# The second batch's attention on 64x64 matmuls, with its x read back from DRAM

## Chip, cores and metric

The kernel runs on one core of one Trainium2 chip. The metric is device time in microseconds, the median of several executions of the whole program.

## What is computed

Linear attention, then two dense layers, in float32. The inputs have 8 batches of 576 tokens and 8 heads of 64.

```python
kv = einsum('bhsd,bhse->bhde', k, v)
out = einsum('bhsd,bhde->bhse', q, kv)
x = out / sqrt(mean(out*out, axis=-1) + 1e-6) * g_norm     # to 4608 tokens x 512
x = square(maximum(x @ moe_w_in, 0)) @ moe_w_out           # 512 -> 2048 -> 512
h = x @ moe2_w_in
y = (h * cos(h)) @ moe2_w_out
```

## The kernel before, in words

A large matmul is made of three matmuls on operands that are split into a high and a low part (`h` by a cast to the matmul's reduced type, `l` by a subtraction): high by high, high by low, low by high.

The first layer's first part goes over tiles of `TOK` = 512 tokens, `t` = 0 to 8, and in each over 8 **chunks** of 128 hidden units, numbered through as chunk 0, 1, 2 and so on. `layer_in` (L370) computes a chunk's hidden units with 12 matmuls of 128x512 (L379); ScalarE and VectorE apply relu and square and split the result (`act_relu2`, its relu at L388 frees the PSUM bank `l`, its last step at L394 makes `gl`); two chunks later `layer_out` (matmuls L416) multiplies by the second weights, again 12 matmuls. So a chunk is 24 matmuls. The rest of the program (the other hidden units of layer one, and layer two, lines from 430 on) begins after these chunks.

Attention is computed batch by batch between the chunks. For batch `b`, 40 small matmuls (`kv_mm`, L258) make `kv`. Then come 8 **units** `(b, p, i)`: `p` is one of 4 pairs of heads. `att_a` (L278) multiplies q by kv into two `o` banks, `att_o` squares (L299) and scales (L300), `att_b` sums the squares over a head with a matmul by ones into the bank `ss` and takes the reciprocal root (L319, L321), `att_c` makes the normalized piece `xo` with three VectorE operations (L329 to L331), and `att_e` (L351) writes `xo` to DRAM (`x_d`) on GpSimd's queue. There are two ways through this:

- For `b < NEXACT` (before: batches 0 and 1) `att_a` uses one block-diagonal 128x128 float32 matmul for each half of the tokens (L288), and `att_b` one float32 matmul (L314). `att_d` (L334) casts and splits `xo` directly into `xh`, `xl` of the first `NDIRECT` tiles (L348, L349).
- For later batches `att_a` uses four 64x64 matmuls for each `p` (L292), one for each quarter of the array: two heads by two halves of the tokens. `sq` is split into `sh` and `sl` (L306, L307), and `att_b` takes two matmuls in the reduced type (L316, L317). `load_x` (L224) reads x back from `x_d` in two halves of the model dimension, `q` = 0 and 1, into a tile `xraw`, and `split_x` (L229) casts and splits it in four pieces `c` of 512 columns (L232, L233).

A table of jobs says after which chunk number each piece is asked for: `starts` gives, for each batch, the chunk number of its first unit and the step between units (L730); `at(n0 - ..., load_x, ...)` and `at(..., split_x, ...)` do so for x (L744 to L749). A scheduler then orders the instructions of each engine; each engine keeps that order, and a DMA queue issues in order too.

Of the kernel before, what the change touches and what calls it, by code (L numbers as in the profile page):

```python
# [8 lines left out]
F32 = mybir.dt.float32  # L9
# [7 lines left out]
P = 128  # L17
# [5 lines left out]
def kernel(  # L23
# [17 lines left out]
    NKC = DM // P  # L41
    NF = wA.shape[0]
    NH = NF // 2
    NP = NH // 2
    NEXACT = 2
    NQ = 3
    NRAW = 4
    KVB = 5
# [4 lines left out]
    TOK = 512  # L53
# [2 lines left out]
    TILES = [(0, 512), (BIG, 512), (2 * BIG, 512), (3 * BIG, 384), (3 * BIG + 768, 384)]  # L56
    assert sum(2 * ht for _, ht in TILES) == NT
    LAG = 2
    NDIRECT = 2
    EPS = 1e-6  # L60
    NSC = (S + P - 1) // P
    NPR = 7
# [28 lines left out]
    def bank(use):  # L91
        tag = banks[use].pop(0)
        banks[use].append(tag)
        return bank_tile(tag)

    def as32(ap):
        return ap.bitcast(F32)
# [111 lines left out]
    xraw = {}  # L209
# [6 lines left out]
    def pieces(first, count, size):  # L216
        done = 0
        while done < count:
            b, s = divmod(first + done, size)
            n = min(count - done, size - s)  # L220
            yield b, s, done, n
            done += n

    def load_x(t, q):  # L224
        raw = xraw[t, q] = x_p.tile([P, 2, TOK], F32, tag="xr", name="xraw", bufs=2)
        for b, s, done, n in pieces(t * TOK, TOK, S):
            nc.sync.dma_start(out=raw[:, :, done:done + n], in_=x_d[b][:, 2 * q:2 * q + 2, s:s + n])

# [49 lines left out]
    def att_a(*u):  # L278
# [6 lines left out]
        os = [bank("o")[:, :HS] for _ in range(2)]  # L285
        if b < NEXACT:
            for o, half in zip(os, halves):
# [8 lines left out]
    def att_o(o, *u):  # L296
# [3 lines left out]
        nc.scalar.activation(out=og, in_=o, func=AF.Copy, scale=gcol)  # L300
        if u[0] < NEXACT:
            att[u] = (og, sq, None)
# [7 lines left out]
    def att_b(*u):  # L310
        og, sh, sl = att[u]
        ss = bank("ss")[:, :HS]
        if u[0] < NEXACT:
            nc.tensor.matmul(ss, as32(ones[:]), sh[:], start=True, stop=True)  # L314
# [19 lines left out]
    def att_d(*u):  # L334
        b, p, hf = u
        xo = att[u]
        if b >= NEXACT:
            return
        tok = b * S + hf * HS
        for t in range(NDIRECT):  # L340
            lo, hi = max(tok, t * TOK), min(tok + HS, (t + 1) * TOK)
# [9 lines left out]
    def att_e(*u):  # L351
        b, p, i = u
        xo = att.pop(u)
        if b < NEXACT:
            nc.gpsimd.dma_start(out=x_d[b][:, p, i * HS:(i + 1) * HS], in_=xo)
# [319 lines left out]
    def at(n, fn, *a):  # L675
        jobs.append((n, len(jobs), fn, a))
# [50 lines left out]
    late_stream.place([pos(n) for n in (0.95, 2.5, 3.25, 4.5, 6.4, 8.7, 10.75)], 0)  # L727

    kv_stream = Stream(load_kv, kv_mm, [(b, c) for b in range(B) for c in range(NSC)])
    starts = [(-13, 1), (-3, 0.8)] + [(-3 + 7 * (b - 1), 7 / (2 * NKC)) for b in range(2, B)]  # L730
    kv_stream.place([s0 - 0.5 for s0, _ in starts for c in range(NSC)], 0)
    q_items = [(b, p) for b in range(B) for p in range(NKC)]
    for b, (s0, ds) in enumerate(starts):
        for i, u in enumerate(att_units(b)):
# [8 lines left out]
            at(n + 2.5, att_e, *u)  # L743
    for t in range(NDIRECT, NTILE):  # L744
        n0 = t * NH
        for q in range(2):
            at(n0 - (6.2, 3 if t == 2 else 4.2 if t == 3 else 5.1)[q], load_x, t, q)
        for c in range(NKC):
            at(n0 - 3.2 + 0.8 * c, split_x, t, c)  # L749


    PH = 1 / 7
# [184 lines left out]
```

## Time and profile before

| | |
|---|---|
| Median of 3 runs | 1575.07 us (1573.13 to 1575.84) |
| The profiled execution's own time | 1573.13 us |
| Its span, first to last instruction | 1571.4 us |
| TensorE busy in the span | 1536.6 us (98%) |
| VectorE, ScalarE, GpSimd busy | 82%, 68%, 7% |
| Mean granted TensorE clock | 0.998 |

The profiled execution is 1.94 us shorter than the median. Matmul times in the rows overlap, since one starts before the one ahead of it has ended: what a matmul costs is read from start to start, not from its duration. A float32 matmul stands as two instructions in the trace, so that "x2" can be one matmul. In a row of the timeline the brackets tell how long the engine was idle before it, and who ended that.

### The profile page before, as it was taken

The numbers are of one execution on the slowest core, as the hardware profiler recorded it, in microseconds if no ns is written. First come the engines' busy times: TensorE is split into PE (matmuls) and PEld (weight loads), VectorE is DVE, ScalarE is ACT, GpSimd is POOL, SyncE is SP. The second block draws the span as 40 slices with busy tenths as digits, with TensorE's granted clock in tenths as the row PEclk, the third lists the DMA queues.
The fourth block names the chain that finished last, engine by engine and source line by source line (L and its number), as shares of the span: only waits on it lengthen the run. The fifth ranks groups of instructions, "written<-read, shape, count | busy, mean of one in ns | idle before, by whom it ended". The sixth has DMA issues, their size and how long they took to land.

```text
span 1571.4 us, 24645 instructions
## 1 busy us (share of the span) xinstructions
PE 1536.6 (98%) x9104; PEld 1347.5 (86%) x9104; DVE 1294.0 (82%) x1744; ACT 1074.5 (68%) x1528; POOL 108.4 (7%) x171
## 2 busy tenths in 40 slices
PE   5999999999999999999999999999999999999998
PEld 4777777778888888888998899999999999999998
DVE  7987878888875899998979779867986788779777
ACT  5977767785434766656556777777777777777774
POOL 1112111110000000000000000000000000001000
PEclk9999999999999999999999999999999999999999
DMA  9858888877578979898997978887888789999995
GB/s 320 283 161 234 273 266 249 251 215 225 170 235 282 334 241 370 304 382 281 383 351 279 343 215 255 254 282 215 255 248 282 215 248 276 305 322 292 303 308 149
DMA packets 222151, 426.31 MB, mean 271 GB/s; under 512 B 18000, under 2 KB 138064, under 8 KB 222032
## 3 DMA queue, kind: packets, MB, share of 16 engines
q1 hardware_dynamic: 210560, 390.13, 73.2%
q0 software_dynamic: 11472, 34.61, 10.3%
q8 instruction: 73, 1.20, 0.3%
q14 instruction: 46, 0.38, 0.1%
HBM read 317.72 MB, written 81.79 MB: 254 GB/s over the span
## 4 chain that ended last, share of the span: by engine, by line
PE 80%; DVE 8%; DMA 7%; ACT 3%; issue 2%; SPq 0%; POOL 0%; DVEq 0%; ACTq 0%; POOLq 0%
PE SB L629 15%; PE FA L505 15%; PE FB L505 15%; PE SA L629 15%; PE acc L416 10%; PE l L379 8%; DMA ws_d<-raw 2%; DMA wi<-wi_d 1%; PE o L379 1%; PE ss L379 1%; DVE gl L606 1%; DMA xraw<-x_d 1%; DMA q<-in_qT 1%; DVE sum L657 1%; DMA sum<-part 1%
## 5 line engine op out<-in xcount | busy, mean ns | idle before, releaser
L505 PE MATMUL FA<-xh,wi 128*128 128x512 f32 (+1 forms) x840 | 302.7, 371 | 3.9 <-DVE h L534 2.8
L505 PE MATMUL FB<-xh,wi 128*128 128x512 f32 (+1 forms) x840 | 301.8, 370 | 0.0
L629 PE MATMUL SA<-ws,gh 128*128 128x256 f32 x1008 | 233.1, 280 | 0.4 <-ACT y L564 0.4
L629 PE MATMUL SB<-ws,gh 128*128 128x256 f32 x1008 | 233.1, 280 | 0.2 <-ACT part L654 0.2
L629 PEld LDWEIGHTS SA<-ws,gh 128*128 128x128 f32 x1008 | 183.6, 188 | 13.3 <-ACT y L564 0.5
L629 PEld LDWEIGHTS SB<-ws,gh 128*128 128x128 f32 x1008 | 183.3, 188 | 12.2 <-ACT part L654 0.4
L505 PEld LDWEIGHTS FA<-xh,wi 128*128 128x128 f32 x840 | 157.6, 189 | 14.2 <-DVE h L534 3.1
L505 PEld LDWEIGHTS FB<-xh,wi 128*128 128x128 f32 x840 | 157.3, 188 | 9.6
L606 DVE TENSOR_TENSOR gl<-y,gh 128x1024 fp32r<-128x1024 f32 (+1 forms) x100 | 111.5, 1114 | 40.5 <-ACT gh L605 40.3
L629 PE MATMUL SB<-ws,gl 128*128 128x256 f32 x504 | 141.3, 280 | 1.1 <-DVE gl L606 1.1
L629 PE MATMUL SA<-ws,gl 128*128 128x256 f32 x504 | 141.2, 280 | 0.5 <-DVE gl L606 0.5
L572 DVE SCALAR_TENSOR_TENSOR y<-y,h 128x1024 f32<-128x1024 f32 (+1 forms) x80 | 89.2, 1115 | 47.5 <-ACT y L568 47.3
L655 POOL DMA_DIRECT2D sum<-part x53 | 45.7, 862 | 1140.6 <-DMA ws<-ws_d 584.4
L554 ACT ACTIVATE y<-h,zerob 128x1024 int32<-128x1024 f32 (+1 forms) x80 | 85.0, 1063 | 50.3 <-DVE h L530 50.3
L416 PE MATMUL acc<-gh,wh 128*128 128x512 f32 x288 | 113.6, 396 | 0.0
L416 PE MATMUL acc<-gl,wh 128*128 128x512 f32 x288 | 112.9, 392 | 0.0
L416 PE MATMUL acc<-gh,wl 128*128 128x512 f32 x288 | 112.6, 391 | 0.0
L505 PE MATMUL FA<-xl,wi 128*128 128x512 f32 (+1 forms) x300 | 111.0, 370 | 0.0
L505 PE MATMUL FB<-xl,wi 128*128 128x512 f32 (+1 forms) x300 | 110.9, 370 | 0.0
L629 PE MATMUL SA<-gh,ws 128*128 128x512 f32 (+1 forms) x280 | 101.0, 369 | 0.6 <-ACT xh L478 0.6
L564 ACT ACTIVATE y<-y 128x1024 f32<-128x1024 f32 (+1 forms) x80 | 78.1, 976 | 34.0 <-DVE y L558 33.9
L629 PEld LDWEIGHTS SB<-ws,gl 128*128 128x128 f32 x504 | 94.9, 188 | 7.4 <-DVE gl L606 1.5
(171 smaller groups left out, 3820.6 us busy)
## 6 DMA issues: line engine op xcount, KB each, us to landing
wi<-wi_d SPq DMA_DIRECT2D x210, 512.0 KB, 6.4
ws<-ws_d SPq DMA_DIRECT2D x210, 512.0 KB, 5.3
sum<-part POOLq DMA_DIRECT2D x33, 512.0 KB, 7.3
kvld<-in_kv SPq DMA_DIRECT2D x32, 512.0 KB, 6.3
ws_d<-raw SPq DMA_DIRECT2D x24, 448.0 KB, 4.2
q<-in_qT SPq DMA_DIRECT2D x32, 288.0 KB, 4.8
p_d<-ev SPq DMA_DIRECT2D x18, 512.0 KB, 4.0
raw<-in_wA SPq DMA_DIRECT2D x16, 512.0 KB, 7.2
```

The costliest lines, as they stand in the source:

```text
L379: nc.tensor.matmul(ps, a[:, 0, cs], m[:], start=(c == 0 and k == 0), stop=(c == NKC - 1 and k == 2))
L416: nc.tensor.matmul(o, a[:, cs], m[:], start=(f == 0 and n == 0), stop=(f == NH - 1 and n == 2), skip_group_check=True)
L505: nc.tensor.matmul(ps[:, pp, :], a, b, start=(n == 0 and (i in (0, 2) or i == 1 and not seeded(k))), stop=(n == 5), skip_group_check=True,)
L554: nc.scalar.activation(out=y.bitcast(I32), in_=hs[k, b], func=AF.Identity, bias=zerob)
L564: nc.scalar.activation(out=y, in_=y, func=AF.Sin, scale=math.pi)
L572: nc.vector.scalar_tensor_tensor(out=y, in0=y, scalar=-2.0 * math.pi, in1=hs.pop((k, b)), op0=ALU.add, op1=ALU.mult)
L606: nc.vector.tensor_tensor(out=l, in0=src, in1=as32(h), op=ALU.subtract)
L629: nc.tensor.matmul(ps[:, b, :], lhs, rhs, start=(n == 0 and (m == 0 or b % 2 == 0) and i in (0, 1, 2)), stop=(n == 5), skip_group_check=True,)
L655: nc.gpsimd.dma_start(out=e, in_=part, accum_op=ALU.add)
L657: nc.vector.tensor_tensor(out=e, in0=ps, in1=e, op=ALU.add)
```

## The change

`NEXACT` and `NDIRECT` go from 2 to 1: batch 1 takes the 64x64 way, and the second tile's x (`t` = 1) is read back from `x_d` and split by `split_x`. Its `xraw` lies in the pool `ev`, which otherwise serves the results of `layer_out`. Batch 1's units are asked for 0.75 chunks apart instead of 0.8; batch 2 starts at chunk 5.5 with a step of 0.65, where it started at chunk 4 with 0.875. The loads of x get other leads for the tiles 1 and 2, and the four splits of every tile are asked for 2.4, 1.8, 1.2 and 0.6 chunks ahead of the tile, where they were asked for 3.2, 2.4, 1.6 and 0.8 ahead.

```diff
-    NEXACT = 2
+    NEXACT = 1
-    NDIRECT = 2
+    NDIRECT = 1
...
     def load_x(t, q):
-        raw = xraw[t, q] = x_p.tile([P, 2, TOK], F32, tag="xr", name="xraw", bufs=2)
+        if t == NDIRECT:
+            raw = ev_p.tile([P, 2, TOK], F32, tag="ev", name="xraw")
+        else:
+            raw = x_p.tile([P, 2, TOK], F32, tag="xr", name="xraw", bufs=2)
+        xraw[t, q] = raw
...
-    starts = [(-13, 1), (-3, 0.8)] + [(-3 + 7 * (b - 1), 7 / (2 * NKC)) for b in range(2, B)]
+    starts = [(-13, 1), (-3, 0.75), (5.5, 0.65)] + [(-3 + 7 * (b - 1), 7 / (2 * NKC)) for b in range(3, B)]
...
         for q in range(2):
-            at(n0 - (6.2, 3 if t == 2 else 4.2 if t == 3 else 5.1)[q], load_x, t, q)
+            lead = {1: (5.5, 3.2), 2: (5.6, 3), 3: (6.2, 4.2)}.get(t, (6.2, 5.1))
+            at(n0 - lead[q], load_x, t, q)
         for c in range(NKC):
-            at(n0 - 3.2 + 0.8 * c, split_x, t, c)
+            at(n0 - (2.4, 1.8, 1.2, 0.6)[c], split_x, t, c)
```

The lines of the changed file lie 4 or 5 further down: L292 of before is L296 there, L388 is L392, L416 is L420.

The scheduler's order of the instructions shows what moves. The first place is TensorE between the second product of chunk 4 and the first of chunk 6, where one head pair of batch 2 is multiplied. Before:

```order
L416 MATMUL acc_805<-gl,wh 128x512
L416 MATMUL acc_805<-gh,wl 128x512
L292 MATMUL l_1109<-q,kvx_137 64x288
L292 MATMUL o<-q,kvx_137 64x288
L292 MATMUL l_1109<-q,kvx_137 64x288
L292 MATMUL o<-q,kvx_137 64x288
L416 MATMUL acc_793<-gh,wh 128x512
```

With the change:

```order
L296 MATMUL l_1182<-q,kvx_137 64x288 x2
L420 MATMUL acc_816<-gh,wh 128x512
L383 MATMUL l_1094<-xh,wh 128x512
L383 MATMUL l_1094<-xl,wh 128x512
L320 MATMUL ss<-sh,ones 128x288
L420 MATMUL acc_816<-gl,wh 128x512
L420 MATMUL acc_816<-gh,wl 128x512
L296 MATMUL o<-q,kvx_137 64x288
L383 MATMUL l_1094<-xh,wl 128x512
```

The four 64x64 matmuls of a head pair stood next to each other, in every batch that took this way; in batches 1 and 2 of the changed kernel the same four stand as two and one and one, with 128x512 matmuls between them (the last `o` comes some ten rows later). From batch 3 on they stand in fours again, and from chunk 10 on all engines' orders are those of before.

The second place is ScalarE at the end of batch 0, where the last two pieces of the first tile's x are cast for chunk 0 (`xh<-xo 128x288`, then `128x224`). Before:

```order
L348 CAST xh<-xo 128x288
L205 CAST wh<-w 128x512
L319 ACTIVATE r<-acc_553,epsb 128x288
L299 ACTIVATE sq<-o 128x288
L348 CAST xh<-xo 128x224
```

With the change:

```order
L304 ACTIVATE og<-acc_499,gcol 128x288
L310 CAST sh<-sq 128x288
L303 ACTIVATE sq<-acc_500 128x288
L304 ACTIVATE og<-acc_500,gcol 128x288
L352 CAST xh<-xo 128x288
L310 CAST sh<-sq 128x288
L303 ACTIVATE sq<-o 128x288
L352 CAST xh<-xo 128x224
```

Two casts of batch 1's squares stand ahead of that piece now, and one reciprocal root of batch 1 has moved behind it.

The third place is ScalarE ahead of the relu of chunk 6 (`r<-l_1094`, before `r<-l_1076`). Before:

```order
L348 CAST xh<-xo 128x160
L300 ACTIVATE og<-o,gcol 128x288
L388 ACTIVATE r<-l_1076 128x512
L390 ACTIVATE g<-r 128x512
L393 CAST gh<-g 128x512
```

With the change:

```order
L205 CAST wh<-w 128x512
L236 CAST xh<-xraw 128x512 x2
L392 ACTIVATE r<-l_1094 128x512
L303 ACTIVATE sq<-o 128x288
L394 ACTIVATE g<-r 128x512
```

The two casts that read the second half of tile 1's x from its DRAM load stand directly ahead of the relu. The casts of the first half stand in the same way ahead of chunk 4's relu.

## Rows read from the trace of the kernel before

**Rows 1.** The page's head and its busy times over the whole span.
```profile
span 1571.4 us, 24645 instructions
PE 1536.6 (98%) x9104; PEld 1347.5 (86%) x9104; DVE 1294.0 (82%) x1744; ACT 1074.5 (68%) x1528; POOL 108.4 (7%) x171
```
**Rows 2.** Windows: stretch, its length, busy us and instructions of each engine, clock, DMA.
```profile
25.00:45.00 20.00, 15.76 (x125) 10.98 (x123) 18.96 (x48) 18.17 (x52) 4.54 (x8) 0.91 0.96 323
45.00:62.00 17.00, 16.77 (x140) 13.35 (x139) 16.47 (x38) 14.29 (x33) 2.39 (x4) 1.00 0.75 257
62.00:111.00 49.00, 49.00 (x238) 36.91 (x240) 43.94 (x94) 41.84 (x93) 7.71 (x14) 1.00 0.59 191
```
**Rows 3.** Timeline of TensorE, 37 to 111 us: start, length, instruction, idle before.
```profile
37.86 0.75 PE L314 MATMUL ss<-sq,ones 128*128 128x288 f32 x2 [1.81 <-ACT sq L299]
...
43.59 0.49 PE L379 MATMUL l<-xh,wh 128*128 128x512 f32 x1 [0.41 <-ACT xh L348]
...
44.86 0.61 PE L379 MATMUL acc<-xh,wh 128*128 128x512 f32 x1
...
61.99 0.50 PE L379 MATMUL l<-xh,wh 128*128 128x512 f32 x1 [0.23 <-ACT r L388]
...
110.73 2.70 PE L258 MATMUL l<-kvld 128*64 128x64 f32 x80
```
**Rows 4.** Timeline of TensorE around one exact 128x128 attention matmul (L288).
```profile
50.81 0.39 PE L379 MATMUL l<-xh,wl 128*128 128x512 f32 x1
51.05 0.65 PE L288 MATMUL o<-q,kvx 128*128 128x288 f32 x2
51.31 0.60 PE L416 MATMUL acc<-gh,wh 128*128 128x512 f32 x1
51.76 0.39 PE L416 MATMUL acc<-gl,wh 128*128 128x512 f32 x1
```
**Rows 5.** Timeline of TensorE around four 64x64 attention matmuls (L292).
```profile
78.14 0.39 PE L416 MATMUL acc<-gh,wl 128*128 128x512 f32 x1
78.46 0.45 PE L292 MATMUL l<-q,kvx 64*64 64x288 f32 x1
...
78.76 0.40 PE L292 MATMUL l<-q,kvx 64*64 64x288 f32 x1
...
79.11 0.50 PE L416 MATMUL acc<-gh,wh 128*128 128x512 f32 x1
79.44 0.39 PE L416 MATMUL acc<-gl,wh 128*128 128x512 f32 x1
```
**Rows 6.** Timeline of TensorE around one pair of sums of squares, high and low.
```profile
84.99 0.30 PE L316 MATMUL ss<-sh,ones 128*128 128x288 f32 x1
85.12 0.29 PE L317 MATMUL ss<-sl,ones 128*128 128x288 f32 x1
85.26 0.39 PE L416 MATMUL acc<-gh,wh 128*128 128x512 f32 x1
```
**Rows 7.** Timeline of ScalarE: last casts for chunk 0, relus of chunks 5 and 6.
```profile
43.08 0.60 ACT L348 CAST xh<-xo 128x224 fp32r<-128x224 f32 x2
...
76.66 0.58 ACT L388 ACTIVATE r<-l 128x512 f32<-128x512 f32 x1
...
81.24 0.42 ACT L306 CAST sh<-sq 128x288 fp32r<-128x288 f32 x1
...
84.05 0.60 ACT L388 ACTIVATE r<-l 128x512 f32<-128x512 f32 x1 [0.56 <-PE l L379]
```
**Rows 8.** Waits (us in total, times, longest): ScalarE 20:200, TensorE 25:350.
```profile
ACT xh L232 <- DMA xraw<-x_d: 6.3, 3, 2.7
PE l L379 <- ACT r L388: 1.7, 3, 1.0
```
**Rows 9.** DMA issues, 20 to 200 us: count, KB each, median us to landing.
```profile
x_d<-xo POOLq DMA_DIRECT2D x39, 72.0 KB, 3.2
...
xraw<-x_d SPq DMA_DIRECT2D x2, 384.0 KB, 6.6
```

## The prediction

> **What bounds the kernel now.** I read the busy times first: TensorE is busy for 1536.6 of 1571.4 us, so 34.8 us are left in all, and whatever the change gives or costs has to show as TensorE work or as TensorE waiting [rows 1]. The windows come next, over the part that the change touches [rows 2]. From 25 to 45 us TensorE has 15.76 of 20 us, while VectorE (18.96) and ScalarE (18.17) are nearly full: these two set the pace of the start. From 45 to 62 us all three are close to full (16.77, 16.47, 14.29 of 17). From 62 to 111 us TensorE is busy all 49 us, VectorE 43.94 and ScalarE 41.84: here TensorE alone sets the pace. The timeline of TensorE gives the marks: a wait of 1.81 us for a square and of 0.41 us for the last cast of chunk 0, chunk 1 at 44.86, chunk 3 at 61.99 after a wait of 0.23 us, and batch 3's kv at 110.73 [rows 3]. From chunk 10 on the order is that of before on every engine, so what TensorE has lost or won by then is what the end of the program should show.
>
> **Prices on TensorE, from start to start.** A 128x512 matmul takes 0.23 us (50.81 to the next start at 51.05, rounded). With one exact matmul L288 among two of these, 50.81 to 51.76 is 0.95, so the exact one costs 0.49 [rows 4]; L314, of the same size and passes, is taken at the same. Four 64x64 matmuls together: 78.14 to 79.44 is 1.30 with two of 0.23 in it, so 0.84 for the four [rows 5]. A pair of sums, high and low, starts at 84.99 and the next matmul at 85.26: 0.27 [rows 6].
>
> What no row shows is a 64x64 matmul or two that stand alone between full ones; call such a piece a set. From below it is 0.49, since a set streams as many columns in as many passes as one exact matmul [rows 4]; from above it is the four's 0.84 [rows 5]. I take 0.75. In the four, the second pass starts 0.30 after the first (78.46, 78.76), so some 0.24 of the 0.84 is entry and exit: the first L292 comes 0.32 after the matmul ahead of it, and the second matmul after the group starts 0.33 after the first (79.11, 79.44), both instead of 0.23. A lone set has to go in and out as well, so it is nearer the four: 0.49 and about a quarter. TensorEngine Tiling (Array Packing) of the Trainium skill, under Key Properties, says that a change of the tiling mode drains TensorE; the late starts on both sides of the group agree with it. TensorE: Matmul & The Clock Gate of the Trainium skill, in Part 3, says that a single small matmul takes the time of a full one and that only concurrency gains; by that alone a set would be 0.49, and the sum below 4.2 us instead of 6.3.
>
> **The change, part by part.**
>
> 1. Chunk 1 starts later, **+0.9 us** (-0.5 to +1.5). The order ahead of the last cast for chunk 0 has two more casts of squares (0.42 each by the row at 81.24) and one reciprocal root less (about 0.4); VectorE has two more subtractions there, which wait for those casts and hold back the pieces that ScalarE waits for (0.1 to 0.3). In before that last cast begins at 43.08 and TensorE waits for it [rows 3, 7]. That is +0.6; ahead of chunk 1 then stands a set (0.75) in place of an exact matmul (0.49), +0.3. The four 64-column casts of batch 0 that fall away are no gain here, as the engine is then waiting for VectorE. From below, a gain of 0.5, if they do count.
>
> 2. Batch 1 on TensorE from chunk 1 to its end, **0**. Before: 2 L288 and 6 L314, 8 x 0.49 = 3.9. Changed: 3 sets and 6 pairs, 3 x 0.75 + 6 x 0.27 = 3.9. (-0.8 with sets of 0.49, +0.2 with 0.84.) The rest of batch 1 lies ahead of chunk 1, where TensorE waits anyway. In fours the same batch would have been a clear gain; the split eats it.
>
> 3. Queueing between 45 and 62 us, **+0.7 us** (0 to 2). ScalarE and VectorE are close to full, and in this stretch they get the `sh` and `sl` of batch 1 before they have lost the `xh`, `xl` of the direct way, some three more VectorE operations ahead of chunk 1's `gl`. TensorE's kv matmuls of batch 2 and its chunk 3 stand behind a bank that ScalarE frees; in before it already waits 0.23 there [rows 2, 3].
>
> 4. Batch 2 on TensorE, **+3.75 us** (2.45 to 4.2). In before its four head pairs are four groups of four; in the changed order they are nine sets, five more, 5 x 0.75. They fall into the stretch in which TensorE has no idle time [rows 2], so nothing covers them. The sums of squares stay as they were.
>
> 5. Two new waits of ScalarE for a load of x, **+1.0 us** (0 to 4). Tile 1's second half can only be loaded when the last unit of batch 1 is in DRAM: 3.2 us from issue to landing, then about 6.6 us for a load of 448 KB, taken from the 384 KB row [rows 9], 9.8 us in all. On ScalarE the two casts of it stand directly ahead of chunk 6's relu, while the VectorE order puts that unit's `xo` just ahead of chunk 5's `gl`; from chunk 5's relu to chunk 6's are 7.4 us [rows 7]. So ScalarE waits some 2 us, and all behind it, the relu first. The direct way had no such wait; the three that tiles 2 and 3 have now sum to 6.3 us, while TensorE's waits for a relu sum to 1.7 [rows 8]. I pass a quarter on: 0.6 here, 0.4 for the first half.
>
> 6. At nothing: the casts and subtractions of `split_x` replace those of `att_d`, a net 2 to 3 us more on each of ScalarE and VectorE, which have 7 and 5 us free from 62 to 111 [rows 2]; without that cover they would be a term like part 3. GpSimd issues 8 more DMAs, SP 4 more; GpSimd is 7% busy [rows 1], and SP's wait for batch 1's writes holds back loads of q, kv and weights that have a buffer's time in hand. The wider step between batches 1, 2 and 3 moves no work off TensorE.
>
> Sum: 0.9 + 0 + 0.7 + 3.75 + 1.0 = **6.3 us slower**, by the bounds 1.1 to 11.9. The sum is made against the profiled execution, 1573.13 us, which gives 1579.5; that execution lies 1.94 us under the median, so on the median of 1575.07 the forecast is **1581.4 us**.
>
> **The rivals.**
>
> - *Splitting costs little.* Lone sets at 0.49, no new queueing, the loads in time: parts 2 and 4 become -0.8 and +2.45, and with +0.5 of part 1 the sum is about +2: 1577.2 us. For it speaks that no row shows a lone set; against it the entry and exit of the four.
> - *The load of x decides.* One place, the casts ahead of chunk 6's relu: with ScalarE 2.4 us late, two casts of 0.6 behind that, and then the scaling that frees TensorE's `o` bank some six instructions on, TensorE stops for 3 to 4 us more instead of 0.6: about +10, 1585 us. It decides as soon as the load lands over 3 us after ScalarE has come to it, the length of the 12 matmuls (12 x 0.23) that lie between a relu and the next chunk. The longest such wait now is 2.7 us [rows 8].
> - *Faster.* Batch 1's exact matmuls go and the sets hide beside their neighbours, so that batch 1 is 16 x 0.49 = 7.8 against 4 x 0.84 + 8 x 0.27 = 5.5, -2.3; batch 2 stays as it was; and the waits at the start (1.81 and 0.41, [rows 3]) go with the direct casts, -2.2. Sum -4.5: 1570.6 us. It needs a lone set to cost under 0.3 and the start not to be later. TensorEngine Tiling (Array Packing) of the Trainium skill, under Theoretical Speedup, promises up to 2 times for a dimension of 64, which speaks for this rival; the four show less, 0.84 against two exact ones at 0.98 [rows 4, 5].
>
> **How the numbers follow.** About 0.2%, 3.15 us, is what a measurement of this kernel can tell from no change. The forecast (+3.2 to +8) has 0.42, the late load (+8 to +12 and a little over) 0.23, little cost (-3.1 to +3.1) 0.25, faster 0.10. So slower 0.65, same 0.25, faster 0.10. The range runs from 1573.5 (most of "little cost") to 1587.5 (the upper bound of the sum, 1575.07 + 11.9, rounded up); it leaves out the faster case and a twentieth above.
>
> **What would show it.** In the profile after: L296 in lone sets, with the next 128x512 starting about 0.75 + 0.23 after the one ahead of the set; chunk 1 near 45.8, chunk 3 near 63.6, batch 3's kv near 117; ScalarE's cast from `xraw` waiting for a DMA twice before 95 us; the later course shifted by the same amount. The forecast is wrong if lone sets start and end without a gap, if chunk 1 is earlier than 44.9, or if the shift at batch 3's kv isn't found again at the end.

## The result and the profile after

The changed kernel takes 1591.80 us (median of 5 runs, 1590.49 to 1596.71) against 1574.28 us for the kernel before in the same job (5 runs): a ratio of 1.0111, 95% interval 1.0098 to 1.0124, or 17.5 us slower. The forecast was 1581.4 us with a range of 1573.5 to 1587.5: the sign is right, the size is not.

The page's head and busy times of the changed kernel, which answer to [rows 1]:

```profile
span 1594.6 us, 24700 instructions
PE 1554.4 (97%) x9120; PEld 1352.9 (85%) x9120; DVE 1297.3 (81%) x1744; ACT 1076.7 (68%) x1528; POOL 112.2 (7%) x179
```

TensorE is busy 17.8 us longer with 16 more instructions. The windows of [rows 2] again, for the changed kernel (stretch, its length, busy us and instructions of each engine, granted clock, DMA):

```profile
25.00:45.00 20.00, 15.47 (x114) 8.68 (x115) 15.60 (x37) 13.90 (x36) 3.44 (x6) 0.78 0.78 271
45.00:62.00 17.00, 17.00 (x51) 9.44 (x50) 11.74 (x27) 11.43 (x30) 3.35 (x6) 0.66 0.79 233
62.00:111.00 49.00, 44.54 (x249) 31.20 (x248) 38.47 (x80) 34.90 (x74) 6.56 (x12) 0.93 0.58 179
```

Between 45 and 62 us TensorE is busy all the time, while VectorE (16.47 us before) and ScalarE (14.29 us), which were close to full, now have a third of that stretch free. The column that explains it is the clock: 0.66 where [rows 2] has 1.00. Cut more finely, with the same columns, the low stretch is

```profile
36.00:40.00 4.00, 1.61 (x7) 0.96 (x6) 3.96 (x10) 1.94 (x5) 1.08 (x2) 0.94 0.23 88
40.00:56.00 16.00, 16.00 (x43) 7.15 (x43) 8.18 (x21) 10.94 (x29) 2.29 (x4) 0.50 0.84 260
56.00:60.00 4.00, 4.00 (x18) 3.32 (x17) 4.00 (x10) 3.32 (x8) 0.00 (x0) 0.93 0.52 148
...
88.00:92.00 4.00, 3.60 (x9) 2.95 (x10) 4.00 (x8) 3.06 (x7) 0.82 (x2) 0.50 0.35 121
```

and in the kernel before

```profile
40.00:56.00 16.00, 15.59 (x67) 11.96 (x66) 15.33 (x35) 15.22 (x38) 2.17 (x4) 1.00 0.88 298
```

For 16 us on end TensorE runs at the lower of its two levels, 1.2 GHz (0.50), with no idle time in the profile, and gets through 43 instructions where it did 67. A second, shorter fall lies at 88 to 92 us. The marks on TensorE's timeline, as in [rows 3] (start, length, instruction, idle before):

```profile
35.64 0.40 PE L383 MATMUL l<-xh,wl 128*128 128x512 f32 x1
38.42 0.50 PE L383 MATMUL l<-xh,wh 128*128 128x512 f32 x1 [2.38 <-ACT xh L352]
38.76 1.38 PE L292 MATMUL acc<-q,kvx 128*128 128x288 f32 x4
39.93 1.30 PE L318 MATMUL ss<-sq,ones 128*128 128x288 f32 x2
41.16 1.22 PE L296 MATMUL acc<-q,kvx 64*64 64x288 f32 x2
...
54.09 0.80 PE L383 MATMUL acc<-xh,wh 128*128 128x512 f32 x1
...
74.22 0.50 PE L383 MATMUL l<-xh,wh 128*128 128x512 f32 x1 [0.99 <-ACT r L392]
...
88.40 0.61 PE L320 MATMUL ss<-sh,ones 128*128 128x288 f32 x1 [3.14 <-DVE m L333]
...
131.53 0.91 PE L262 MATMUL l<-kvld 128*64 128x64 f32 x22
```

Chunk 1 begins 9.2 us later than in [rows 3], chunk 3 12.2, batch 3's kv 20.8, and the span is 23.2 us longer (this execution, 1596.71 us, is the longest of its five). So most of the loss is made in the first 130 us. Two things lead the rows. At 38.42 a matmul of chunk 0 (its c = 2) waits 2.38 us for a cast, and it stands ahead of the last exact q·kv of batch 0, which ran at about 35 us before. I had not read that in the order. And at 88.40 TensorE waits 3.14 us for VectorE. The reason for the second is on ScalarE, as the forecast's part 5 had it, but at chunk 4 and not at chunk 6:

```profile
85.78 0.62 ACT L236 CAST xh<-xraw 128x512 fp32r<-128x512 f32 x1 [3.71 <-DMA xraw<-x_d]
86.31 0.61 ACT L205 CAST wh<-w 128x512 fp32r<-128x512 f32 x1
86.83 0.61 ACT L236 CAST xh<-xraw 128x512 fp32r<-128x512 f32 x1
87.35 0.72 ACT L112 ACTIVATE e<-e,expb 128x512 int32<-128x512 int32 x1
87.97 0.57 ACT L392 ACTIVATE r<-l 128x512 f32<-128x512 f32 x1
```

These are ScalarE's rows: it waits for tile 1's x, and the cast `wh`, for which VectorE waits ahead of its `m`, and chunk 4's relu come after it.

### The profile page after: what moved, and what is told of

The parts are those of the page before. It is cut to its first block, busy times and chain, and to the rows that moved or that the text cites. A ratio compares the mean times of both kernels' runs of the same rounds, so it can differ in the third digit from the quotient of the medians.

```text
span 1594.6 us, 24700 instructions
## 1 busy us (share of the span) xinstructions
PE 1554.4 (97%) x9120; PEld 1352.9 (85%) x9120; DVE 1297.3 (81%) x1744; ACT 1076.7 (68%) x1528; POOL 112.2 (7%) x179
## 4 chain that ended last, share of the span: by engine, by line
PE 83%; DMA 7%; DVE 6%; issue 2%; ACT 2%; SPq 0%; POOL 0%; DVEq 0%; ACTq 0%; POOLq 0%
PE SB L633 15%; PE FB L509 15%; PE SA L633 15%; PE FA L509 15%; PE acc L420 10%; PE l L383 8%; DMA raw<-in_wB 1%; DMA xraw<-x_d 1%; PE o L383 1%; DMA ws_d<-raw 1%; PE ss L383 1%; PE o L296 1%; DMA q<-in_qT 1%; DMA sum<-part 1%; DMA x_d<-xo 1%
## 5 line engine op out<-in xcount | busy, mean ns | idle before, releaser
L420 PE MATMUL acc<-gl,wh 128*128 128x512 f32 x288 | 112.9, 392 | 0.0
L420 PE MATMUL acc<-gh,wl 128*128 128x512 f32 x288 | 112.6, 391 | 0.0
L420 PE MATMUL acc<-gh,wh 128*128 128x512 f32 x288 | 112.2, 395 | 0.0
L383 PE MATMUL l<-xh,wh 128*128 128x512 f32 x240 | 98.1, 409 | 4.8 <-ACT xh L352 2.8
```

The lines of the kernel that those rows point to most:

```text
L383: nc.tensor.matmul(ps, a[:, 0, cs], m[:], start=(c == 0 and k == 0), stop=(c == NKC - 1 and k == 2))
L420: nc.tensor.matmul(o, a[:, cs], m[:], start=(f == 0 and n == 0), stop=(f == NH - 1 and n == 2), skip_group_check=True)
```

## The experiments

Twelve kernels, each against the kernel before in its own job. "Chunk 1" and "kv 3" are the starts of chunk 1's first matmul and of batch 3's kv in the profiled execution. That is one execution of each kernel: the longest one for the changed kernel and runs 1, 2 and 3, the shortest one for the kernel before and run 4.

| run | what | median us | against before (95%) | chunk 1 | kv 3 |
|---|---|---|---|---|---|
| | before [rows 3] | 1574.28 | 1 | 44.86 | 110.73 |
| | changed | 1591.80 | 1.0098 to 1.0124 | 54.09 | 131.53 |
| 1 | start's order put back | 1590.12 | 1.0056 to 1.0128 | 53.06 | 132.40 |
| 2 | TensorE kept busy in the wait | 1586.12 | 1.0040 to 1.0085 | 49.51 | 123.69 |
| 3 | batch 1 exact, x through DRAM | 1578.84 | 1.0010 to 1.0030 | 46.72 | 116.25 |
| 4 | timing alone | 1580.19 | 1.0015 to 1.0040 | 45.02 | 113.98 |
| 5 | casts of x later | 1591.13 | 1.0083 to 1.0113 | 54.78 | 127.55 |
| 6 | 2 and 5 together | 1582.39 | 1.0032 to 1.0061 | 47.26 | 118.58 |
| 7 | leads and splits alone | 1575.58 | 0.9990 to 1.0007 | 45.81 | 111.71 |
| 8 | 3 and 5 together | 1578.87 | 1.0013 to 1.0032 | 49.36 | 116.68 |
| 9 | batch 1's q·kv full-array only | 1582.73 | 1.0034 to 1.0064 | 49.00 | 119.75 |
| 10 | batch 1 later | 1582.21 | 1.0033 to 1.0062 | 36.43 | 120.61 |
| 11 | before, fours cut in two | 1588.81 | 1.0067 to 1.0101 | 45.37 | 116.00 |
| 12 | timing, third batch as before | 1577.72 | 1.0000 to 1.0023 | 46.21 | 114.15 |

**Run 1: the order at the start.** In the changed kernel (`last_qkv` holds the last matmul of L292):

```diff
         for c in range(NKC):
+            with tc.issue_after(last_qkv[0].ins) if len(fs) > 1 and c > 1 else ExitStack():
                 xh, xl = xs[t, c]
```

> The changed kernel, with one order put back: the matmuls of chunk 0 with x of c = 2 and 3 are queued behind the last exact q.kv matmul of batch 0, as they stood before. Theory A (the start's order, and the fall of TensorE's clock behind it, is the largest part): the last q.kv of batch 0 runs at about 35 us instead of 38.76, the granted clock does not stay at 0.50 from 40 to 56 us, chunk 1's first matmul comes at 45 to 48 us instead of 54.09, and the time is 1581 to 1585 us. Rival B (the order is worth only the idle time that ends in it, 2.4 us, and the rest is the added work of batch 1's quarter path): chunk 1's first matmul at 51 to 53 us, time 1589 to 1591 us. Rival C (the x load and the timing decide, the start does not): chunk 1 earlier, but the time stays at 1590 to 1592 us, because a later wait takes it up.

The order came as wanted (the q·kv at 35.95), but in the profiled execution, the longest of the six, theory A does not hold: chunk 1 is at 53.06 and the clock is low all the same, behind a wait of only 1.66 us. The window of run 1, with the columns as above:

```profile
36.00:40.00 4.00, 2.34 (x9) 1.01 (x7) 3.96 (x10) 2.99 (x8) 1.08 (x2) 1.00 0.62 183
40.00:56.00 16.00, 16.00 (x42) 7.92 (x42) 9.09 (x23) 10.71 (x28) 2.29 (x4) 0.51 0.71 240
```

But the six executions of this one kernel divide by the clock: three had a mean granted clock of 0.998 or 0.999 and spans of 1580.3 to 1584.2 us, three had 0.989 to 0.992 and 1592.0 to 1595.7. Only one of the second group was profiled. Read by their mean clocks, the fall is not certain in this order, and where it comes it goes with some 12 us; the times of the first group (1582.1 to 1586.2 us) are about where theory A had them, and the median of 1590.12 lies between the groups. The changed kernel's five executions have 0.989 to 0.995. So the order seems to matter for whether the clock falls, and the question became what keeps it down.

**Run 2: TensorE busy during the wait.**

```diff
+            if len(fs) > 1 and c == 2:
+                for _ in range(12):
+                    nc.tensor.matmul(pss[0], wts[0, fs[0]][0][:, 0, cs], xh[:], start=False, stop=False)
             xh, xl = xs[t, c]
```

> The changed kernel with 12 more matmuls of chunk 0's form (128x128 by 128x512, operands that are there already) between those of c = 1 and c = 2, in the stretch in which TensorE waits for the cast of c = 2; chunk 0's sums hold extra products, so the output is not the reference's. The last q.kv of batch 0 stands behind them and starts at about 38.4 us, no earlier than in the changed kernel (38.76). Theory A, clock part (the wait costs most by the lower clock that follows it): the granted clock is 1.0 from 40 us on, chunk 1's first matmul comes at 46 to 49 us, and the time is 1583 to 1588 us although work was added. Rival B (the idle time and the late q.kv themselves cost it, the clock follows from the waiting of TensorE on ScalarE and VectorE): chunk 1's first matmul at 53 to 56 us, time 1591 to 1594 us.

The windows of run 2, same columns:

```profile
36.00:40.00 4.00, 4.00 (x14) 3.15 (x13) 3.92 (x9) 1.15 (x3) 0.96 (x2) 0.69 0.24 94
40.00:56.00 16.00, 15.86 (x71) 9.00 (x69) 11.52 (x27) 14.55 (x37) 2.29 (x4) 1.00 0.84 285
```

The last q·kv of batch 0 starts at 40.09, later than in the changed kernel, and chunk 1 still comes 4.6 us earlier; the clock is 1.00 and TensorE does 71 instructions in the 16 us where it did 43. The time is 5.7 us lower although work was added. The clock part of theory A holds; chunk 1 at 49.51 is just outside what it gave. The 64x64 matmuls are all still there: at 1.00, they do not bring the clock down by themselves.

**Run 3: batch 1 exact again, all else as changed.**

```diff
-    NEXACT = 1
+    NEXACT = 2
```

> The changed kernel with batch 1's attention on the exact full-array path again (both heads in one matmul, the sum of squares in one float32 product), while x of tile 1 still goes through DRAM and the new starts, leads and split times stay. What it takes back is the quarter path alone. Theory A: the matmul of chunk 0's c = 2 still stands ahead of batch 0's last q.kv, so the start's loss stays for the most part: chunk 1's first matmul at 49 to 53 us; about 16 lone 64x64 sets of 0.82 us are gone against 8 exact ones of 0.49, and the time is 1583 to 1588 us. Rival D (the quarter path of batch 1 is the cost as such): 1575 to 1579 us. Rival C (the load of x through DRAM is the cost): 1589 to 1592 us.

Here the same matmul of chunk 0 stands ahead of the q·kv and waits 2.20 us, and the clock falls too. But it comes back soon:

```profile
36.00:40.00 4.00, 3.06 (x7) 2.16 (x8) 2.68 (x6) 1.49 (x4) 0.54 (x1) 0.61 0.12 46
40.00:56.00 16.00, 14.81 (x61) 10.99 (x60) 13.67 (x30) 14.66 (x37) 2.16 (x4) 0.99 0.96 325
```

The time is 13 us lower than the changed kernel's and in rival D's range: the quarter path as such. Chunk 1 comes earlier than theory A gave. (The expectation counted some 16 lone sets for batch 1; its order has eight pieces.) What follows the wait thus matters more than the wait. Run 9 makes that sharper.

**Run 9: only the four 64x64 matmuls of batch 1 made two full-array ones.**

```diff
-        if b < NEXACT:
+        if b < 2:
             for o, half in zip(os, halves):
                 nc.tensor.matmul(o, kvs[b][:, p, :], q[:, half], start=True, stop=True)
```

> The changed kernel, with the four 64x64 matmuls of batch 1's head pairs replaced by the two exact 128x128 ones, and nothing else: its sums still go as high and low pairs, x of tile 1 still through DRAM, starts and leads are the new ones, and the matmul of chunk 0's c = 2 still stands ahead of batch 0's last q.kv. The rows of o then hold heads where batch 1's later steps expect halves, so its part of the output is mixed up. Theory A' (it is the 64x64 matmuls behind the wait at 36 to 38 us after which TensorE's clock stays at 1.2 GHz for some 16 us; behind full-array matmuls it comes back, as in the third run, where 36 to 40 us had 0.61 and 40 to 44 us 0.96): the granted clock is back at 1.0 by 48 us, chunk 1's first matmul comes at 46 to 50 us and the time is 1580 to 1585 us. Rival J (the wait alone, or the pairs of sums with their casts on ScalarE, keep it low): the clock stays at 0.50 until 52 us or later, chunk 1 at 52 to 55 us, 1588 to 1592 us.

TensorE's timeline of run 9:

```profile
38.65 0.50 PE L383 MATMUL l<-xh,wh 128*128 128x512 f32 x1 [2.53 <-ACT xh L352]
38.99 1.51 PE L292 MATMUL acc<-q,kvx 128*128 128x288 f32 x4
40.30 1.17 PE L318 MATMUL ss<-sq,ones 128*128 128x288 f32 x2
41.26 1.17 PE L292 MATMUL acc<-q,kvx 128*128 128x288 f32 x2
...
49.00 0.60 PE L383 MATMUL acc<-xh,wh 128*128 128x512 f32 x1
```

Its windows:

```profile
36.00:40.00 4.00, 1.47 (x6) 0.88 (x5) 3.96 (x11) 1.86 (x5) 1.08 (x2) 0.95 0.25 97
40.00:44.00 4.00, 4.00 (x13) 2.93 (x11) 1.15 (x3) 3.21 (x9) 0.00 (x0) 0.62 0.61 194
44.00:56.00 12.00, 10.98 (x47) 8.36 (x47) 11.75 (x28) 12.00 (x32) 2.41 (x4) 1.00 0.98 335
```

The wait is even a little longer than in the changed kernel (2.53 against 2.38), the first rows after it are the same ones at the same low level (L292 1.51, L318 1.17), and by 44 us the clock is back. The first thing that differs is what comes at 41: a full-array L292 here, an L296 of 64x64 there. Theory A' holds, rival J falls, and the exchange is worth 9.1 us (1591.80 to 1582.73; 10.3 if each is taken against the kernel before in its own job). Not all of that is the first fall. TensorE's later wait for VectorE has shrunk as well, and no second fall follows:

```profile
78.83 0.40 PE L320 MATMUL ss<-sh,ones 128*128 128x288 f32 x1 [1.34 <-DVE m L333]
```

And the 64x64 matmuls are dearer even at full clock: batch 1's eight pieces at 0.83 (run 11 below) against eight exact matmuls at 0.49 [rows 4] are an estimated 2.7 us. That leaves some 6.4 for the clock. The mean granted clocks of the two median executions give about the same: 0.991 leaves 0.009 of a span of 1589.8 us, 14.3 us, and 0.995 leaves 0.005 of 1580.7 us, 7.9 us. It is an estimate, and of the medians only: the shortest of the changed kernel's five executions has 0.995 too and still took 1590.49 us, and it was not profiled.

**Run 5: the casts of tile 1's x behind later relus.**

```diff
-        nc.scalar.copy(out=h, in_=src)
+        with tc.issue_after(relus[(5, 5, 7, 7)[c]].ins) if t == 1 else ExitStack():
+            nc.scalar.copy(out=h, in_=src)
```

> The changed kernel with one order edited: the four casts of tile 1's x are queued on ScalarE behind the relus of chunks 5, 5, 7 and 7 instead of ahead of the relus of chunks 4 and 6. Nothing is left out. Theory F (the wait of ScalarE for x through DRAM, 3.71 us at 85.78, holds the relu, the cast of w and with them TensorE, 3.14 us, and lets its clock fall a second time): no wait of TensorE over 1 us between 80 and 100 us, granted clock 1.0 there, time 1584 to 1588 us. Rival G (the load is late for whatever stands there, or TensorE waits for the next thing, VectorE's m, at the same place): 1590 to 1593 us. The first fall of the clock, at 40 us, stays in both.

In the trace it did what theory F said. From run 5's windows:

```profile
40.00:56.00 16.00, 16.00 (x43) 6.97 (x42) 7.31 (x20) 10.86 (x29) 1.87 (x4) 0.50 0.81 254
84.00:96.00 12.00, 12.00 (x59) 8.76 (x58) 11.85 (x25) 9.32 (x20) 2.77 (x6) 1.00 0.79 241
```

There is no second fall and no idle time from 84 to 96 us, and kv 3 comes 4.0 us earlier than in the changed kernel although chunk 1 comes 0.7 later. But the median, 1591.13, is only 0.7 us lower, which is rival G's range and not theory F's. The two profiled spans differ by 4.6 us, the five runs of each overlap. So alone it isn't shown to gain.

**Run 6: run 2 and run 5 together.** The two edits above.

> The 12 added matmuls of the second run and the later casts of tile 1's x together (chunk 0's sums hold extra products, so the output is not the reference's). Theory F with A's clock part (each fall of the clock has its own price, and they add): granted clock 1.0 from 40 to 100 us and 1579 to 1583 us, near the 1579 to 1580 that the exact batch 1 and the timing alone gave. Rival G (with the start repaired, the x load costs nothing more): 1585 to 1588 us, as the second run.

Run 6 has no window below 1.00 between 36 and 96 us:

```profile
36.00:40.00 4.00, 3.98 (x17) 2.55 (x15) 3.41 (x8) 2.39 (x7) 0.54 (x1) 1.00 0.26 83
40.00:56.00 16.00, 15.87 (x72) 9.40 (x71) 13.78 (x32) 15.18 (x40) 3.35 (x6) 1.00 0.98 324
...
84.00:96.00 12.00, 12.00 (x50) 7.65 (x49) 10.67 (x21) 10.42 (x23) 0.00 (x0) 1.00 0.52 152
```

At 1582.39 us it is 3.7 us below run 2 and within theory F's numbers, but the intervals of the two runs overlap: what the load of x costs in the changed kernel lies between 0.7 and 4.6 us (runs 5, 6 and the spans), and no run settles it better. What run 6 shows is the change without its falls of the clock, with 12 matmuls added and the casts of x moved: +7.0 us.

**Runs 4, 7, 12 and 3 beside each other: the rest.** Run 4 is the kernel before with the new numbers of the table (the diff), run 7 the same without its line of starts, so with the new leads and splits alone.

```diff
-    starts = [(-13, 1), (-3, 0.8)] + [(-3 + 7 * (b - 1), 7 / (2 * NKC)) for b in range(2, B)]
+    starts = [(-13, 1), (-3, 0.75), (5.5, 0.65)] + [(-3 + 7 * (b - 1), 7 / (2 * NKC)) for b in range(3, B)]
-            at(n0 - (6.2, 3 if t == 2 else 4.2 if t == 3 else 5.1)[q], load_x, t, q)
+            lead = {2: (5.6, 3), 3: (6.2, 4.2)}.get(t, (6.2, 5.1))
+            at(n0 - lead[q], load_x, t, q)
-            at(n0 - 3.2 + 0.8 * c, split_x, t, c)
+            at(n0 - (2.4, 1.8, 1.2, 0.6)[c], split_x, t, c)
```

Run 12 is run 4 with the third batch as before:

```diff
-    starts = [(-13, 1), (-3, 0.75), (5.5, 0.65)] + [(-3 + 7 * (b - 1), 7 / (2 * NKC)) for b in range(3, B)]
+    starts = [(-13, 1), (-3, 0.75), (4, 7 / (2 * NKC))] + [(-3 + 7 * (b - 1), 7 / (2 * NKC)) for b in range(3, B)]
```

Expected of run 4:

> The kernel before with only the numbers of the change's table: batches 1 and 2 start at -3 with 0.75 and at 5.5 with 0.65, and the leads of the loads and splits of x are the new ones for tiles 2 and up; batch 1 stays exact and goes straight into tile 1's x. Theory A: here batch 0's last q.kv stands ahead of chunk 0's c = 2 as before, so chunk 1's first matmul comes at 45 to 47 us and the time is 1571 to 1577 us. Rival E (the later third batch and the later splits are what costs): 1583 to 1592 us.

Expected of run 7:

> The kernel before with only the new leads of the loads of x and the later split times for tiles 2 and up; the batches start as before. The timing alone gave 1580.19 us against 1575.45. If the later casts and loads are its part (theory H): 1578 to 1582 us, with a wait of TensorE or ScalarE for x at chunks 16, 24 or later. If batch 2's start 1.5 chunks later is (theory I): 1573.5 to 1576.5 us, as before.

Expected of run 12:

> The fourth run's kernel (the kernel before with the new starts, leads and split times) with batch 2 started at 4 with the old step again instead of at 5.5 with 0.65. In the fourth run's order batch 2's four head pairs are six pieces (4, 2, 2, 1, 1, 2 and a 4); here they are five (4, 2, 2, 4, 4). Theory I (the later third batch costs the 4.7 us, by its extra sets, some 0.8 each, and by the banks that it holds at chunk 3): 1574.5 to 1577 us. Rival H' (batch 1's shorter step and the new split times do it): 1578.5 to 1581.5 us, as the fourth run.

Theory A missed run 4: chunk 1 is where it said (45.02), but the time is 4.7 us over before. Theory I holds in run 7: the leads and splits cost nothing that can be measured (0.1 us). Run 12 falls between its two ranges: putting the third batch back takes 2.9 of the 4.7 us, each measured against before in its own job, and 1.9 stay (with an interval from 0 to 3.6). In the scheduler's order batch 2's four fours are seven pieces in run 4 (not six, as the expectation says), five in run 12, four in runs 3 and 7, and nine in the changed kernel and in run 9. The times follow that count roughly: from run 3 to run 9, five more pieces and pairs of sums in batch 1 are +3.9 us. But run 3, in fours, lies 3.2 us above run 7, also in fours, so x through DRAM, with the new start and the later third batch, has its price too; no run parts these.

**Run 8: run 3 with the later casts.** The edits of runs 3 and 5.

> The third run's kernel (batch 1 exact, x of tile 1 through DRAM) with the four casts of tile 1's x queued behind the relus of chunks 5, 5, 7 and 7. In its trace ScalarE waits 2.67 us for x at 73.57 and TensorE 1.99 us behind it at 76.19. Theory F: this wait of TensorE is gone and the time is 1575.5 to 1577.5 us against 1578.84. Rival G: 1578 to 1580 us.

Rival G holds: no gain, 1578.87. TensorE's wait is gone, but batch 2 is six pieces instead of four, and one wait at the start grew to 3.56 us.

**Run 11: the price of a lone set.** In the kernel before the four matmuls are issued half by half:

```diff
-            for half, part in zip(halves, heads):
-                for o, r in zip(os, heads):
-                    nc.tensor.matmul(o[part], kvs[b][r, p, r], q[r, half], start=True, stop=True, skip_group_check=True)
+            half_of(halves[0], heads[0])
+            pending.append(rest)
+            return
...
+            while pending:
+                pending.pop(0)()
```

The last two lines stand in `layer_in` behind the three matmuls of each c; `rest` issues the second half and then `att_o`.

> The kernel before with each of the 24 groups of four 64x64 matmuls (batches 2 to 7) cut in two: the first half's pair stays, the second half's pair is issued behind the first three matmuls of the next chunk step. On TensorE 24 fours become 50 lone sets, nearly all in stretches where TensorE has no idle time. It measures the price of a lone set, for which the forecast took 0.75 between 0.49 and 0.84, the four at 0.84. By 0.82, as the sets of the changed kernel read at full clock: 50 x 0.82 - 24 x 0.84 = 20.8 us, 1593 to 1599 us. By 0.49 (a lone set takes the time of one exact matmul): 50 x 0.49 - 20.2 = 4.3 us, 1578 to 1582 us.

TensorE's timeline of run 11 around one such set:

```profile
139.33 0.40 PE L390 MATMUL l<-xh,wl 128*128 128x512 f32 x1
139.65 0.45 PE L294 MATMUL o<-q,kvx 64*64 64x288 f32 x1
139.66 0.45 PE L294 MATMUL l<-q,kvx 64*64 64x288 f32 x1
139.95 0.40 PE L294 MATMUL o<-q,kvx 64*64 64x288 f32 x1
139.95 0.40 PE L294 MATMUL l<-q,kvx 64*64 64x288 f32 x1
140.28 0.50 PE L390 MATMUL l<-xh,wh 128*128 128x512 f32 x1
140.62 0.40 PE L390 MATMUL l<-xl,wh 128*128 128x512 f32 x1
```

From 139.33 to 140.62 is 1.29, with two of 0.23 in it: 0.83 for a pair, where [rows 5] gives 0.84 for four. Half the work takes the same time. In the changed kernel a single one, at full clock, takes it too (102.52 less 101.23 is again 1.29; "x2" is one matmul):

```profile
101.23 0.40 PE L420 MATMUL acc<-gh,wl 128*128 128x512 f32 x1
101.56 0.69 PE L296 MATMUL o<-q,kvx 64*64 64x288 f32 x2
102.18 0.50 PE L383 MATMUL l<-xh,wl 128*128 128x512 f32 x1
102.52 0.39 PE L383 MATMUL l<-xh,wh 128*128 128x512 f32 x1
```

By that price 26 more sets are 21.6 us; the median rose by 13.2 (10.6 to 15.9), and the two profiled spans differ by 15.9. In the kernel before, TensorE's waits between 60 and 365 us (us in total, times, longest) are the 1.7 us of [rows 8] and

```profile
PE ss L316 <- DVE m L329: 4.6, 5, 1.3
```

and in run 11 all of them are

```profile
PE ss L327 <- ACT sh L317: 0.4, 1, 0.4
PE l L390 <- ACT r L401: 0.2, 1, 0.2
PE ss L328 <- DVE sl L318: 0.2, 1, 0.2
```

so 5.5 us of waiting went, as TensorE became slower than its suppliers. Between the two profiled executions that covers it: 21.6 less 5.5 is 16.1. A set of 0.83 cost this kernel 0.5 to 0.6 on average, because part of it filled waits; that it costs its full price where there are none was not measured by itself. Neither of the two expected ranges holds.

**Run 10: a version that might beat both.**

```diff
-    starts = [(-13, 1), (-3, 0.75), (5.5, 0.65)] + [(-3 + 7 * (b - 1), 7 / (2 * NKC)) for b in range(3, B)]
+    starts = [(-13, 1), (-1.5, 0.55), (5.5, 0.65)] + [(-3 + 7 * (b - 1), 7 / (2 * NKC)) for b in range(3, B)]
-            lead = {1: (5.5, 3.2), 2: (5.6, 3), 3: (6.2, 4.2)}.get(t, (6.2, 5.1))
+            lead = {1: (5.2, 3), 2: (5.6, 3), 3: (6.2, 4.2)}.get(t, (6.2, 5.1))
```

with run 5's edit.

> A try at a version that beats both: the changed kernel with batch 1 started at -1.5 with steps of 0.55 instead of at -3 with 0.75, tile 1's loads of x led by 5.2 and 3 instead of 5.5 and 3.2, and its casts behind the relus of chunks 5, 5, 7 and 7. Six matmuls of chunk 0 and 1 more stand ahead of batch 0's last q.kv then, and 10 lone sets of batch 1 are left instead of 16. If the 64x64 matmuls only cost where TensorE waits (theory A'): the granted clock stays at 1.0 from 44 us on and the time is 1572 to 1580 us. If they cost wherever they stand (their lone sets, and the clock): 1582 to 1590 us.

The clock stays at 1.00 through the start, as theory A' has it; chunk 1 begins at 36.43, with its first six matmuls ahead of batch 0's last q·kv, so that this mark can't be compared with the others. But behind a wait of 2.03 us for a bank, which ends at 64.30, the clock falls (0.50 from 64 to 68 us), and the time of 1582.21 lies in the second range, not in that of theory A'. (Batch 1 is six pieces in its order, eight in the changed kernel's, not the 10 and 16 that the expectation counted.) It is 9.6 us better than the changed kernel and 6.8 us slower than before. No version here beat the kernel before.

## Why the prediction was right or wrong

The steps of the chain from before to changed, each a difference of medians (before stood at 1574.3 to 1575.9 us in the jobs): the new table of starts +4.7 (run 4, of which the leads 0.1), x through DRAM -1.4 (run 3; batch 2 is back in fours there), the pairs of sums in batch 1 and batch 2 in nine pieces +3.9 (run 9), 64x64 matmuls in batch 1 +9.1. They add up to 16.3 of the 17.5 us; the rest is the difference between the jobs. The steps are not independent of each other: the -1.4 holds batch 2's return to fours. The last step is half of the loss, and it is the one that the forecast had at about nothing.

1. *Chunk 1 starts later, +0.9 us (-0.5 to +1.5).* **This is the step that failed.** Measured: +9.2 in the profile. The sum there counted casts on ScalarE and one set, all at full clock. Missed were the matmul of chunk 0 that now stands ahead of batch 0's last q·kv and waits 2.38 us, and above all that TensorE's clock does not come back for 16 us when lone 64x64 matmuls follow that wait. Putting the order back helped only in the three of run 1's six executions whose mean clock stayed up; full-array matmuls in the same place (run 9), or a busy TensorE (run 2), did help. With the clock up chunk 1 still comes 2.4 us later (run 6, with its 12 added matmuls), also more than the bound.
2. *Batch 1 on TensorE, 0.* It was reckoned from chunk 1 on, for three sets; "the rest lies ahead of chunk 1, where TensorE waits anyway" was the wrong cover: at 0.50 that rest was the path. At full clock the set is 0.83, near the upper bound, which would have made this +0.2. The five sets ahead of chunk 1 ran at the low clock.
3. *Queueing, +0.7 (0 to 2).* From chunk 1 to chunk 3 the changed kernel takes 20.1 us against 17.1, partly at the low clock; in run 6 it is 19.0, +1.9, within the bounds.
4. *Batch 2's split sets, +3.75.* The price was nearly right: five more pieces of 0.83 are 4.2 on TensorE. What they cost in time no run shows alone. The nearest is run 6, at full clock: from chunk 3 to batch 3's kv, where all nine pieces lie, it takes 52.3 us against 48.7 before, +3.6. TensorEngine Tiling (Array Packing) of the Trainium skill, Key Properties, has the change of tiling mode drain TensorE; run 11's rows agree: the set starts 0.32 after the matmul ahead of it, and the second full matmul behind it 0.34 after the first, both instead of 0.23. TensorE: Matmul & The Clock Gate of the Trainium skill has, in the table of "Why this matters for your kernels" (the prediction named Part 3), that a single small matmul takes the time of a full one; between full-array matmuls these took 0.83 against 0.49, and the measurement decides.
5. *Two waits for a load of x, +1.0 (0 to 4).* The mechanism is there, at the first half and not the second (3.71 and 0.95 us on ScalarE; the forecast had 2 for the second). TensorE waits 3.14 us behind it and its clock falls again. By the runs it is worth 0.7 to 4.6 us here, and nothing in run 8 against run 3.
6. *At nothing:* the leads and splits, 0.1 (run 7), right. The new starts were at nothing too, but for the pieces that they make of batch 2: with only one piece more, run 12 has +1.9 (0 to 3.6).

The forecast's own marks (chunk 1 near 45.8, chunk 3 near 63.6, batch 3's kv near 117) are missed by the changed kernel. Run 6 comes near them, with 47.26, 66.28 and 118.58 and 1582.39 us in the end: +7.0, where the sum was 6.3. That is in part luck, since parts 1 and 3 are larger there than forecast, while the wait of part 5 is edited away and 12 matmuls are added. What broke the forecast is the 9.4 us between run 6 and the changed kernel, much of it the clock, which was in none of the rivals.

## What to carry to other kernels

Before small-array matmuls are moved to a place where TensorE waits, look at the granted clock there: here it fell behind a wait, and what was issued next made the difference in how soon it came back. A group of matmuls that share the array paid here only where the scheduler kept it together, so count the pieces in the order, and price each piece like the whole group. And a cost that lies in a stretch where an engine waits is covered only as long as the engine's own speed there stays what it was.

## What the runs showed of the hardware

- Behind idle times of 2.20 to 2.53 us, which ended at 36.9 to 38.7 us, the clock fell to 1.2 GHz in runs 3 and 9 and in the changed kernel alike. Behind full-array float32 matmuls it was back by 44 us (run 9: 0.62 at 40 to 44 us, then 1.00); with 64x64 ones among the matmuls it stayed at 0.50 to 56 us, though the profile shows TensorE busy for 16.00 of 16 us. Why it stays was not tested further. Where the clock was up, the same 64x64 matmuls ran at 1.00 (runs 2 and 6).
- The length of the wait alone does not tell whether the clock falls: in run 1's profile it fell behind 1.66 us, in the kernel before it did not behind 1.81 us (1.00 from 36 to 56 us).
- One and the same kernel (run 1) gave spans 12 us apart, with mean granted clocks of 0.998 and of 0.990. In the profiled one the mean is 0.989, and 16 us on end lie at 0.51: an average over the whole span that looks like nothing can hold a whole stage at half speed.
- Between full-array matmuls, one or two 64x64 float32 matmuls take 0.83 us, where four of them take 0.84.
